# Every second piece of the second expert weights split by GpSimd and ScalarE instead of VectorE

## The chip, the cores and the metric

The kernel runs on one core of one Trainium2 chip. Its engines are TensorE (PE in the profile, with its weight loads as PEld), VectorE (DVE), ScalarE (ACT), GpSimd (POOL) and SyncE (SP), which here only issues DMAs. The metric is the device time in microseconds. The kernel before took 1023.83 us as the median of three runs (1018.97 to 1024.21). One execution was profiled; it took 1020.09 us, of which 1018.3 us lie between its first and its last instruction.

## The reference

Three layers follow one another. Attention over 4 batches, 8 heads and 576 positions with a bias made by a small network from the positions; a mixture of 8 experts, in which each token goes to the one expert that it is nearest to; and a feed-forward layer with a squared ReLU.

```python
scores = scale * np.matmul(q, k.transpose(0, 1, 3, 2)) + bias.transpose(2, 0, 1)[None]
attn = softmax(scores); x = (attn @ v) as rows (2304, 512)
for e in range(8):                       # the experts
    h = np.maximum(x[mask] @ w1[e], 0.0)
    out[mask] = gate_w[mask, None] * (h @ w2[e])
h = x @ w_in; g = np.maximum(h, 0.0) ** 2
return g @ w_out
```

The change touches only how `w2` is prepared.

## The kernel before

The kernel is written for one order per engine: each engine runs its instructions in the order in which the program issues them, and waits on semaphores for the others. Attention comes first (roughly 40 to 380 us), then the experts in slots of 128 tokens, then the feed-forward layer.

Attention is one loop over half-steps, `hs`. A half-step is one head of one 128-row block: the scores of head `hs + 1` on TensorE (`emit_qk`, L498), the bias sum and the maximum of head `hs` on VectorE (`emit_max`, L509), the exponential of head `hs - 1` on ScalarE (`emit_exp`, L522), the transposes of head `hs - 3` on TensorE (L531) and their copies out of PSUM (`copy`, L207 on ScalarE or L209 on VectorE), and the product with `v` (L556). The scores have two PSUM buffers, so TensorE can write the scores of head `hs + 1` only once VectorE has read those of head `hs - 1`.

Everything else in that stretch runs as generators, which are resumed once per half-step, at its end: the making of the bias (`bias_group`, whose first ReLU of four goes to GpSimd at L324), the preparation of `q` and `k`, the row sums and the routing of finished rows (`rows`, `route`, L594 to L717), and `presplit`, which is the subject here. A `yield E_` means "go on at the end of the next half-step". Two running totals, `load["A"]` for ScalarE and `load["D"]` for VectorE, stand for the work handed to each engine; they fall by `STEP = 1.95` per half-step. `pick` gives a copy or a ReLU to the engine with the smaller total, `room` holds a generator back while a total would go over `LIM = 2.7`, and `A` and `V` add to a total. So an instruction that is moved from one engine to another also moves copies and ReLUs between VectorE and ScalarE.

`presplit(i)` runs for 32 pieces of `w2`, 128 x 1024 numbers each, and makes of each two half-precision parts, a high one and the remainder: it loads the piece (L465), waits three half-steps, has GpSimd write the high half, `wh[:, 0] = 64 * wr` (L471), waits two half-steps, has VectorE write the remainder, `wh[:, 1] = 64 * wr - wh[:, 0]` (L475), and stores both (L479). There are two `wr` and two `wh` buffers, so two pieces are under way at most. The experts load these parts back later.

## Time and profile before

| what | value |
|---|---|
| median of three runs | 1023.83 us |
| profiled execution | 1020.09 us, span 1018.3 us |
| TensorE busy | 946.7 us (93%) |
| VectorE busy | 662.0 us (65%) |
| ScalarE busy | 540.9 us (53%) |
| GpSimd busy | 499.1 us (49%) |
| L471 on GpSimd | 32 times, 62.2 us |
| L475 on VectorE | 32 times, 47.1 us |

The shares are means over the whole span; the stages differ. The pieces are split between 85 and 345 us, and what the change is worth has to be read there: how busy each engine is in that stretch, and which engine TensorE waits for. Idle time of an engine that nobody waits for costs nothing.

### The profile page before, as it was taken

What the parts mean: (1) busy time and instruction counts of PE and PEld (TensorE: products, weight loads), DVE (VectorE), ACT (ScalarE), POOL (GpSimd) and SP (SyncE); (2) the same over time, 40 slices, a digit from 0 to 9 for tenths busy, and PEclk for the clock granted to TensorE, in tenths of its full rate; (3) what the DMA queues carried; (4) which work ended last, traced back from release to release, by engine and by line L of the source; (5) the groups of instructions that cost most, each with busy time, mean ns of one, the idle gap of its engine ahead of it and who ended that gap; (6) DMA issues with size and microseconds to landing.
All of it is one profiled execution on the core that took longest, in us unless ns stands there. A gap on an engine that the chain in (4) does not pass through costs nothing. (4 is left out here: it accounts for less than half of the span.)

```text
span 1018.3 us, 24810 instructions
## 1 busy us (share of the span) xinstructions
PE 946.7 (93%) x9725; PEld 747.8 (73%) x9725; DVE 662.0 (65%) x1229; ACT 540.9 (53%) x1000; POOL 499.1 (49%) x415
## 2 busy tenths in 40 slices
PE   8687988999899889999999899999999999999995
PEld 4355766677577767776666667688888888888884
DVE  6655899888997874677776767245446455545441
ACT  5666776767777683467565555255423333233330
POOL 1212536446534353366548797275454554645631
PEclk9789999999999999999999999999999999999998
DMA  9998885898779434599899484462011111111000
GB/s 296 318 254 264 305 279 179 267 268 286 226 234 330 163 126 176 213 338 334 325 361 340 146 291 151 153 258 53 22 54 43 32 52 43 32 53 22 22 12 32
DMA packets 78843, 187.17 MB, mean 184 GB/s; under 512 B 26648, under 2 KB 26776, under 8 KB 76128
## 3 DMA queue, kind: packets, MB, share of 16 engines
q1 hardware_dynamic: 72656, 169.98, 49.5%
q0 software_dynamic: 6064, 15.54, 4.4%
q8 instruction: 78, 1.28, 0.5%
q14 instruction: 45, 0.37, 0.1%
HBM read 171.65 MB, written 51.73 MB: 219 GB/s over the span
## 5 line engine op out<-in xcount | busy, mean ns | idle before, releaser
L1436 POOL TENSOR_TENSOR gf<-gf 128x256 f32<-128x256 f32 x144 | 166.0, 1172 | 131.0 <-DVE gf L1433 108.8
L1420 PE MATMUL pf<-big,wih 128*128 128x256 f16 x1728 | 196.0, 273 | 1.5 <-PEq L1374 1.5
L1420 PEld LDWEIGHTS <-wih 128*128 128x128 f16 x1728 | 169.0, 98 | 21.6 <-issue 2.0
L1458 PEld LDWEIGHTS <-g 128*128 128x128 f16 x1512 | 147.4, 98 | 18.7 <-issue 1.0
L1426 ACT ACTIVATE gf<-pf 128x512 f32<-128x512 f32 x72 | 42.5, 597 | 193.3 <-PE pf L1420 140.3
L1220 PE MATMUL ph<-x,w1b 128*128 128x128 f16 x2112 | 127.5, 220 | 7.9 <-DVEq L1024 3.0
L1220 PEld LDWEIGHTS <-w1b 128*128 128x128 f16 x2112 | 122.0, 99 | 13.1 <-DVEq L1024 3.5
L471 POOL TENSOR_TENSOR wh<-wr,w2s_c 128x1024 f16<-128x1024 f32 x32 | 62.2, 1943 | 135.9 <-DMA wr<-in_mw_dram 65.0
L1235 PE MATMUL py<-vt,h 128*128 128x512 f16 x528 | 119.4, 383 | 3.8 <-DMA vt<-wsc 3.8
L1444 DVE TENSOR_TENSOR g<-gf,g 128x1792 f16<-128x1792 f32 x36 | 85.5, 2374 | 50.1 <-ACT g L1443 50.1
L522 ACT ACTIVATE pr<-ssb,mn 128x576 f32<-128x576 f32 x144 | 111.7, 776 | 10.3 <-DVE mn L509 10.3
L509 DVE CUSTOM_DVE_ANT_0 ssb<-ps_s,bias 128x576 f32<-128x576 f32 x144 | 107.4, 749 | 3.1 <-DMA bias<-bias_d 2.2
L1433 DVE TENSOR_TENSOR gf<-gf 128x1024 f32<-128x1024 f32 x28 | 34.3, 1226 | 113.6 <-ACT gf L1426 113.6
L498 PE MATMUL ps_s<-kst,qd 128*128 128x288 f16 (+1 forms) x640 | 96.6, 292 | 11.7 <-DVE mn L509 9.2
L1235 PEld LDWEIGHTS <-h 128*128 128x128 f16 x528 | 51.3, 99 | 63.0 <-issue 7.0
L531 PE MATMUL ps_t<-cst,pr 128*128 128x128 f32 x576 | 92.1, 283 | 2.5 <-DVE pl L607 1.3
L531 PEld LDWEIGHTS ps_t<-cst,pr 128*128 128x128 f32 x576 | 64.9, 144 | 25.7 <-issue 20.8
L556 PE MATMUL pv<-pt,vt 128*64 128x128 f32 (+1 forms) x1280 | 83.6, 274 | 0.0
L498 PEld LDWEIGHTS <-qd 128*128 128x128 f16 (+1 forms) x640 | 56.2, 101 | 26.6 <-issue 16.4
L556 PEld LDWEIGHTS pv<-pt,vt 128*64 128x64 f32 x1280 | 65.5, 140 | 12.5 <-issue 11.4
L1226 DVE SCALAR_TENSOR_TENSOR h<-ph,h 128x512 f16<-128x512 f32 x44 | 30.3, 690 | 49.9 <-ACT h L1225 35.0
L1443 ACT CAST g<-gf 128x1792 f16<-128x1792 f32 x36 | 60.3, 1676 | 4.4 <-POOL gf L1436 4.4
(194 smaller groups left out, 1571.9 us busy)
## 6 DMA issues: line engine op xcount, KB each, us to landing
vt<-wsc SPq DMA_DIRECT2D x88, 512.0 KB
wr<-in_mw_dram SPq DMA_DIRECT2D x76, 512.0 KB
kst<-in_mw_dram SPq DMA_DIRECT2D x44, 512.0 KB
wsc<-wh SPq DMA_DIRECT2D x32, 512.0 KB
bias<-bias_d SPq DMA_DIRECT2D x16, 576.0 KB
bias_d<-rt SPq DMA_DIRECT2D x28, 295.5 KB
qd<-qh SPq DMA_DIRECT2D x64, 128.0 KB
wr<-in_win_dram SPq DMA_DIRECT2D x8, 1024.0 KB
```

The source lines that it names most:

```text
L471: POOL.tensor_tensor(out=wh[:, 0], in0=wr, in1=w2s_c.to_broadcast([P, 1024]), op=ALU.mult)
L498: PE.matmul(s[r, hf, :288], lhsT=qd[:, h2, i, pr, r], rhs=kst[x - x % 2][:, pr, h2, x % 2, js], start=(i == 0), stop=(i == 1))
L509: DVE.tensor_tensor_reduce(out=ss.rearrange("p (a j) -> p a j", a=2), in0=s[:, :, :288], in1=btile[bkey[u]][:, h2].rearrange("p (a j) -> p ...
L522: ACT.activation(pr_sb[k_ // 2][:, h2], ssb.pop(k_), AF.Exp, bias=mns.pop(k_), scale=-1.0, accum_out=sums[c, b][:, h:h + 1])
L531: PE.transpose(pt_ps[k_][:, jc * P:(jc + 1) * P], src[:, j0:j0 + P], eye)
L556: PE.matmul(pv[o, cs], lhsT=vb[:, 2 * jc + h2, d] if jc < 4 else vb[o, 8, d], rhs=a[h2][:, jc, cs] if jc < 4 else e[o, cs], start=(jc == 4 ...
L1220: PE.matmul(p_[:, f4, :], lhsT=w[:, a, kc, f * P:(f + 1) * P], rhs=x2[:, b, kc, :], start=(i == 0), stop=(i == 11))
L1235: PE.matmul(p_, lhsT=h2[:, a, fc, :], rhs=wb2[fc // 2][:, b, fc % 2, :], start=(i == 0), stop=(i == 23))
L1420: PE.matmul(p_[:, h], lhsT=wih[:, a, kc, f * P:(f + 1) * P], rhs=y2[:, b, kc, :], start=(i == 0), stop=(i == 11))
L1436: POOL.tensor_tensor(out=g[:, d], in0=g[:, x], in1=g[:, y], op=op)
L1444: DVE.tensor_tensor(out=gt[:, 1, :, c:c + 2, :], in0=g[:, 1:8], in1=gt[:, 0, :, c:c + 2, :], op=ALU.subtract)
L1458: PE.matmul(ps, lhsT=gt[:, a, s, c, :], rhs=woh[:, c, b, w, :], start=(i == 0 and first), stop=(i == 23 and end), skip_group_check=True)
```

## The change

Pieces of even number go as before, with three differences: the wait after the load is two half-steps instead of three, `room` asks for 1.5 instead of 1.2, and VectorE's total grows as if by 1400 columns instead of 1024. Pieces of odd number go another way: GpSimd multiplies the piece by 64 in place (`wr = 64 * wr`), one half-step later ScalarE copies it into the high half, and GpSimd subtracts the high half from it into the remainder. The wait after the load is two half-steps there too.

```diff
-            for _ in range(3):
+            for _ in range(2):
                 yield E_
             yield from take("wh")
 ...
-            POOL.tensor_tensor(out=wh[:, 0], in0=wr, in1=w2s_c.to_broadcast([P, 1024]), op=ALU.mult)
-            for _ in range(2):
-                yield E_
-            yield from room("D", 1.2)
-            DVE.scalar_tensor_tensor(out=wh[:, 1], in0=wr, scalar=s, in1=wh[:, 0], op0=ALU.mult, op1=ALU.subtract)
-            V(1024)
-            yield E_
+            if i % 2:
+                POOL.tensor_scalar(wr, wr, s, 1.0, op0=ALU.mult, op1=ALU.mult)
+                yield E_
+                yield from room("A", 1.0)
+                ACT.copy(wh[:, 0], wr)
+                A(1024)
+                POOL.tensor_tensor(out=wh[:, 1], in0=wr, in1=wh[:, 0], op=ALU.subtract)
+                yield E_
+                yield E_
+            else:
+                POOL.tensor_tensor(out=wh[:, 0], in0=wr, in1=w2s_c.to_broadcast([P, 1024]), op=ALU.mult)
+                for _ in range(2):
+                    yield E_
+                yield from room("D", 1.5)
+                DVE.scalar_tensor_tensor(out=wh[:, 1], in0=wr, scalar=s, in1=wh[:, 0], op0=ALU.mult, op1=ALU.subtract)
+                V(1400)
+                yield E_
             give("wr")
             SP.dma_start(out=wsc2[i * P:(i + 1) * P, :], in_=wf)
```

The file grows by ten lines, so what stands below the change has a line number that is ten higher after it (L509 becomes L519, L522 becomes L532); of the pieces themselves, L471 becomes L481 and L475 becomes L485, and the new lines are L472 (GpSimd's multiplication in place), L475 (ScalarE's copy) and L477 (GpSimd's subtraction).

TensorE's order doesn't change. On VectorE, counted over the whole program, 16 of the 32 instructions of L475 go; 5 copies of 512 columns, 4 copies `pte` and 5 copies `big` of 128 columns come over from ScalarE, and 3 bias evictions (L335). ScalarE gets 16 copies of 1024 columns and gives up as many of the small ones. GpSimd loses 16 instructions of L471 and gets 16 multiplications and 16 subtractions.

The first place is the routing of the rows of batch group (0, 0), near 150 us. On VectorE, before, from the maximum of one head (L509, with its accumulator read) to the end of the half-step; L651 and L653 are two short steps of the routing.

```order
L509 ISA ssb,mn<-ps_s,bias 128x576
L509 ISA mn 128x1
L475 SCALAR_TENSOR_TENSOR wh<-wr,wh 128x1024
L651 TENSOR_TENSOR z<-z,zm 128x32
L653 TENSOR_SCALAR eq<-z 128x32
```

The same half-step on VectorE now.

```order
L519 ISA ssb,mn<-ps_s,bias 128x576
L519 ISA mn 128x1
L661 TENSOR_TENSOR z<-z,zm 128x32
L663 TENSOR_SCALAR eq<-z 128x32
L326 TENSOR_SCALAR rt<-u_t,bcol 128x320
```

The remainder of an odd piece is gone from before the routing step; a ReLU of the bias has come over from ScalarE behind it.

On ScalarE, before, from the exponential of the next head (L522), with the copies of transposed heads (`pt`, `pte`) and of a finished product (`big`).

```order
L522 ACTIVATE pr,sums<-ssb,mn 128x576
L207 COPY pt<-ps_t 128x512
L207 COPY big<-pv 128x128
L522 ACTIVATE pr,sums<-ssb,mn 128x576
L207 COPY pte<-pv 128x128
```

The same on ScalarE now.

```order
L532 ACTIVATE pr,sums<-ssb,mn 128x576
L207 COPY pt<-ps_t 128x512
L475 CAST wh<-wr 128x1024
L207 COPY big<-pv 128x128
L532 ACTIVATE pr,sums<-ssb,mn 128x576
L207 COPY pt<-ps_t 128x512
```

The copy of an odd piece into its high half now stands ahead of `big` and of the next exponential, and it needs GpSimd's multiplication to be done.

The second place is on GpSimd, a little later: two pieces (L471), the ReLU of a bias group (L324), and the indirect DMAs that write the tokens' places (L701).

```order
L471 TENSOR_TENSOR wh<-wr,w2s_c 128x1024 x2
L324 TENSOR_SCALAR rt<-u_t,bcol 128x304
L701 DMA id_d<-tok,ri 296960x1 x3
L324 TENSOR_SCALAR rt<-u_t,bcol 128x320
L701 DMA id_d<-tok,ri 296960x1
```

The same place on GpSimd now, where L481 is the high half of an even piece, L472 and L477 the multiplication and the subtraction of an odd one, and L711 the indirect DMAs.

```order
L481 TENSOR_TENSOR wh<-wr,w2s_c 128x1024
L472 TENSOR_SCALAR wr<-wr 128x1024
L324 TENSOR_SCALAR rt<-u_t,bcol 128x304
L711 DMA id_d<-tok,ri 296960x1 x2
L477 TENSOR_TENSOR wh<-wr,wh 128x1024
L711 DMA id_d<-tok,ri 296960x1
L324 TENSOR_SCALAR rt<-u_t,bcol 128x320
```

An odd piece now has two instructions on GpSimd, and what stands between and behind them waits for ScalarE's copy as the subtraction does.

## Rows read from the trace of the kernel before

**Rows 1.** Busy time per engine in three stretches (columns: engine busy us, instructions)

```profile
85.00:345.00 260.00, 238.38 (x2637) 176.80 (x2636) 224.08 (x570) 184.67 (x474) 120.63 (x69) 0.99 0.80 258
140.00:160.00 20.00, 15.47 (x170) 11.64 (x170) 19.83 (x38) 12.08 (x33) 8.92 (x5) 1.00 0.74 229
700.00:800.00 100.00, 100.00 (x918) 89.36 (x917) 51.23 (x53) 33.95 (x43) 51.93 (x45) 1.00 0.17 45
```

**Rows 2.** TensorE's waits for VectorE, 85 to 345 us (total, times, longest)

```profile
PE ps_s L498 <- DVE mn L509: 6.7, 7, 2.1
...
PE rk L670 <- DVE oh L662: 2.9, 2, 2.0
PE pv L536 <- DVE big L209: 2.0, 3, 1.2
PE ps_t L531 <- DVE pl L607: 1.3, 1, 1.3
PE ps_t L531 <- DVE pt L209: 1.0, 2, 0.8
```

**Rows 3.** The split's two instructions: busy us, mean ns; for L475 also min/median/max

```profile
L471 POOL TENSOR_TENSOR wh<-wr,w2s_c 128x1024 f16<-128x1024 f32 x32 | 62.2, 1943 | 135.9 <-DMA wr<-in_mw_dram 65.0 <-DMA kst<-wh 32.5 <-DVE pt L209 10.3
L475 DVE SCALAR_TENSOR_TENSOR wh<-wr,wh 128x1024 f16<-128x1024 f32 x32 | 47.1, 1472 | 4.7 <-POOL wh L471 4.7
...
L475 DVE SCALAR_TENSOR_TENSOR wh<-wr,wh x32: 1209/1222/2862, 92.2 to 332.9; 128x1024 f16<-128x1024 f32 x32
```

**Rows 4.** Timeline near 150 us (start us, duration us, engine; idle before in brackets)

```profile
149.62 2.28 POOL L471 TENSOR_TENSOR wh<-wr,w2s_c 128x1024 f16<-128x1024 f32 x1 [4.21 <-DMA wr<-in_mw_dram]
...
150.06 1.88 DVE L651 TENSOR_TENSOR z<-z,zm 128x32 f32<-128x32 f32 x1
...
153.16 0.65 PE L498 MATMUL ps_s<-kst,qd 128*128 128x288 f16 x4 [2.06 <-DVE mn L509]
...
154.80 1.90 POOL L471 TENSOR_TENSOR wh<-wr,w2s_c 128x1024 f16<-128x1024 f32 x1 [0.19 <-DMA wr<-in_mw_dram]
...
154.91 2.86 DVE L475 SCALAR_TENSOR_TENSOR wh<-wr,wh 128x1024 f16<-128x1024 f32 x1
```

**Rows 5.** Two short VectorE operations, each by its line (ns min/median/max)

```profile
L651 DVE TENSOR_TENSOR z<-z,zm x6: 171/187/1884, 150.1 to 398.2; 128x32 f32<-128x32 f32 x3, 128x16 f32<-128x16 f32 x3
...
L326 DVE TENSOR_SCALAR rt<-u_t,bcol x76: 328/464/2011, 5.4 to 278.7; 128x576 f32<-128x576 f32 x6, 128x352 f32<-128x352 f32 x6, 128x560 f32<-128x560 f32 x5, 128x544 f32<-128x544 f32 x5
```

**Rows 6.** Operations like the new ones, from later stages

```profile
L1038 POOL TENSOR_TENSOR xs<-xg,xs 128x512 f16<-128x512 f32 x22 | 28.6, 1302 | 1.8
...
L1037 POOL TENSOR_SCALAR xg<-xg 128x512 f32<-128x512 f32 x22 | 21.8, 990 | 48.7 <-ACT xs L1036 40.5 <-PE ph L1220 7.9
...
L1014 ACT ACTIVATE w1b<-wr x20: 1044/1048/1065, 360.4 to 575.3; 128x1024 f16<-128x1024 f32 x20
```

**Rows 7.** VectorE's groups between 85 and 345 us (busy us, mean ns)

```profile
L509 DVE CUSTOM_DVE_ANT_0 ssb<-ps_s,bias 128x576 f32<-128x576 f32 x109 | 81.4, 748 | 0.6 <-PE ps_s L498 0.5
...
L209 DVE COPY pt<-ps_t 128x512 f32<-128x512 f32 x33 | 22.6, 686 | 13.6 <-PE ps_t L531 13.6
...
L209 DVE COPY pte<-pv 128x128 f32<-128x128 f32 x16 | 4.6, 290 | 3.4 <-PE pv L536 3.1
```

**Rows 8.** Two loads of a piece, each followed by GpSimd's start; GpSimd's wait in total

```profile
158.19 0.43 SPq L465 DMA_DIRECT2D wr<-in_mw_dram  x1
...
162.62 1.90 POOL L471 TENSOR_TENSOR wh<-wr,w2s_c 128x1024 f16<-128x1024 f32 x1 [5.92 <-DMA wr<-in_mw_dram]
...
195.25 0.44 SPq L465 DMA_DIRECT2D wr<-in_mw_dram  x1
...
201.16 1.89 POOL L471 TENSOR_TENSOR wh<-wr,w2s_c 128x1024 f16<-128x1024 f32 x1 [6.17 <-DMA wr<-in_mw_dram]
...
POOL wh L471 <- DMA wr<-in_mw_dram: 65.0, 20, 9.3
```

**Rows 9.** ScalarE's longest wait in total, 85 to 345 us (total, times, longest)

```profile
ACT big L207 <- PE pv L556: 26.6, 35, 7.3
```

## The prediction

> **What bounds the kernel now.** I read the windows first, then TensorE's waits, then the two instructions of the split, then one stall in order of time. After 700 us TensorE is busy without a gap [rows 1], so a microsecond won or lost in attention arrives at the end as it is; nothing there depends on when attention ended. The pieces are split between 85 and 345 us. In these 260 us TensorE is busy 238.4, VectorE 224.1, ScalarE 184.7 and GpSimd 120.6 us [rows 1]. So TensorE bounds the stretch, VectorE is close behind, and only the 260 - 238.4 = 21.6 us in which TensorE idles can be won. The waits say whose they are: for VectorE 6.7 + 2.9 + 2.0 + 1.3 + 1.0 = 13.9 us [rows 2], which is the most that a lighter VectorE can give. They come in clusters: between 140 and 160 us VectorE is busy for 19.83 of 20 us and TensorE for only 15.47 [rows 1].
>
> One cluster shows how they arise [rows 4]. At 149.62 GpSimd starts the high half of a piece. At 150.06 VectorE starts a subtraction of 32 columns, which takes 1.88 us instead of its usual 0.19 [rows 5] and ends within 0.1 us of GpSimd's instruction (149.62 + 2.28 = 151.90). The maximum behind it is late, and TensorE waits 2.06 us for it. At 154.91 the remainder of a piece starts 0.11 us behind another GpSimd instruction and takes 2.86 us. So VectorE is late not only by what it has to do, but also by what GpSimd does beside it.
>
> **The change part by part.** A half-step is 260 / 109 = 2.39 us (109 maxima of L509 in the stretch [rows 7]).
>
> *GpSimd.* Sixteen high halves of 1.943 us go [rows 3], 31.1 us. Sixteen multiplications in place and sixteen subtractions come. The nearest rows have half the columns: 0.990 and 1.302 us [rows 6], doubled 1.98 and 2.60 us, together 16 x 4.58 = 73.3 us. Net +42 us, from 120.6 to 163 us of 260, a third more (35%). There is room for it, so by itself it costs nothing; what it costs is through VectorE and ScalarE, below.
>
> *VectorE.* The remainder takes 1.222 us when nothing is in its way and 1.472 in the mean [rows 3], so (1.472 - 1.222) x 32 = 8.0 of its 47.1 us are delay. Sixteen stay: 16 x 1.222 = 19.6, and half the delay, raised by GpSimd's 35%, 4.0 x 1.35 = 5.4, together 25.0, which is 22.1 less. Against it: five copies of 512 columns at 0.686 and nine of 128 at 0.290 [rows 7], 3.4 + 2.6 = 6.0; three bias evictions, at most 0.686 each, 2.1; and more delay of the short operations that GpSimd holds up, such as the 1.88 and 2.01 us beside medians of 0.19 and 0.46 [rows 5]. How much that is in total no single row says; I take it as large as that of the remainders, 8.0, and 35% of it as added, 2.8. The bounds are 0 and double that. Net 22.1 - 10.9 = 11.2 us less, 5% of 224.1.
>
> The Trainium skill, SBUF — State Buffer, section "SBUF: two separate sides", says that VectorE and GpSimd share one pair of ports as an exclusive lock, that a VectorE operation with two inputs from SBUF and a GpSimd operation that reads SBUF shut each other out for a whole instruction, and that one with its input in PSUM isn't touched. The timeline agrees, with the subtraction that ended with GpSimd's instruction [rows 4]. The rule speaks against this change: an odd piece, which VectorE no longer works on, still shuts VectorE's routing steps out, for longer than before. By the rule the 2.8 us belong in the sum; without it they would be 0, and VectorE 14.0 us lighter.
>
> What that is worth to TensorE: the bounds are 0 and all 13.9 us. Half of the remainders go, so a remainder disappears from ahead of about half of these waits, 6.9 us; 10.9 of the 22.1 us come back in other places, half, and so I take -3.5 us. I don't go further because TensorE is short of work only in clusters, and the routing steps that make them stay where they are.
>
> *ScalarE.* Sixteen copies of 1024 columns at 1.048 us [rows 6] are 16.8 us, less than its idle time of 260 - 184.7 = 75.3 us, part of which goes in copies to VectorE. It is ahead of TensorE much of the time (26.6 us of waiting for a finished product [rows 9]). That cover hides the copies themselves. But each copy is also a new wait. It stands three half-steps behind the load's issue (two after the load, one more after the multiplication), 3 x 2.39 = 7.2 us, unless `room` holds it longer. A piece lands 4.4 to 5.9 us after its issue (162.62 - 158.19 and 201.16 - 195.25 [rows 8]), and the multiplication takes 1.98: 6.4 to 7.9 us. So ScalarE stands still for 0 to 0.7 us at a copy, with the next exponential and the next copy of transposed scores queued behind it, for which TensorE's product with `v` waits. At 0.35 us each that is 5.6 us of ScalarE, of which its lead hides most; I take +1.5 us. Below it is 0; above it is the second rival.
>
> *The queues.* The loads of later pieces are issued by SyncE behind the stores of earlier ones as before; a store of an odd piece now waits for GpSimd instead of VectorE. Behind that store stand loads of bias rows and of `q`, which the program issues 6 and 15 half-steps ahead of their use, and I cost this at 0; without that lead a late store would delay a half-step by as much as GpSimd is late, the second rival's price. The shorter wait after the load makes GpSimd stand waiting for the piece earlier than today, where it waits 65.0 us for pieces already [rows 8]; the ReLU of a bias group behind it starts later, against some half-steps of slack.
>
> *Sum.* -3.5 + 1.5 = -2 us on the profiled execution: 1020.1 - 2 = 1018.1. The median of the three runs is 3.7 us above that execution; I put the base between the two, at 1022, and forecast 1020.
>
> **The rivals.**
>
> *VectorE's waits go nearly all.* For it: VectorE is full just where TensorE stands still, and a cluster goes once VectorE is ahead by its length; the longest wait is 2.1 us [rows 2], less than one delayed remainder of 2.86 [rows 4]. Against it: the routing steps stay, with more GpSimd beside them. Then -13.9 + 1.5 = -12.4, which is 1010.
>
> *GpSimd gets in ScalarE's way.* GpSimd works in order, and a multiplication can stand behind another instruction of the pieces or of a bias group, about 1.94 us (the mean of L471 [rows 3]). Then ScalarE waits 0.35 + 1.94 = 2.3 us at its copy, and with about 1 us hidden by its lead TensorE loses 1.3. It decides as soon as ScalarE waits over 1 us at a copy in the mean. For it: GpSimd's third more work, and the subtraction, which waits for ScalarE in turn, so that each holds up the other. Against it: GpSimd is idle for 260 - 163 = 97 us even then. If half of the copies meet it, 8 x 1.3 = 10.4, and if all do, 21; with VectorE's -3.5 the first is +7, which is 1029, slower than before.
>
> *VectorE gets no lighter.* The delays by GpSimd and the copies that come over take back all 22.1 us: if the short operations lose not 2.8 but 14 us more. Then 0 + 1.5 gives 1023, no change.
>
> **How the numbers follow.** The forecast has a chance of 0.44, with a range of its own from 1015 to 1026; VectorE's waits gone 0.28; GpSimd in ScalarE's way 0.21; VectorE no lighter 0.07. What a measurement of this kernel can tell from no change is about 0.5%, 5 us: the runs before differ by that. Faster by more has the second case and a little of the first, 0.32; slower by more the third and a little of the first, 0.23; within it 0.45. The range takes in most of both sides, 1010 to 1030.
>
> **What would show it.** In the profile of the changed kernel, 16 remainders on VectorE with a mean near 1.5 us; GpSimd near 163 us busy in the same stretch; VectorE 5% less busy there, with TensorE's waits for it near 10 instead of 13.9 us; ScalarE waiting for GpSimd at its new copies, under 1 us each. The forecast is wrong if TensorE's waits for VectorE fall below 5 us, or if ScalarE's waits for GpSimd go over 16 us in total, 1 us per copy.

## The result, and the profile after

The changed kernel takes 1034.03 us, the median of six runs (1030.04 to 1042.68), beside 1021.40 us for the kernel before on the same chip (six runs, 1015.85 to 1024.66): a ratio of 1.0137 over all runs (1.0124 by the medians), with a 95% interval of [1.0106, 1.0167]. The change costs about 13 us; the prediction was 1020 us and its range ended at 1030. The profiled execution took 1032.69 us with a span of 1030.9 us, 12.6 us more than before's 1018.3 us, so it is a fair sample of the difference.

The windows of the changed kernel in the three stretches of [rows 1] come first (engine busy in the order PE, PEld, DVE, ACT, POOL; then the granted clock, DMA share and GB/s).

```profile
85.00:345.00 260.00, 237.81 (x2536) 174.73 (x2535) 203.86 (x536) 186.86 (x454) 138.28 (x82) 0.95 0.81 254
140.00:160.00 20.00, 15.45 (x157) 11.51 (x158) 15.45 (x40) 13.42 (x34) 10.62 (x6) 0.97 0.88 286
700.00:800.00 100.00, 100.00 (x918) 89.45 (x917) 51.02 (x53) 39.59 (x50) 51.72 (x46) 1.00 0.17 44
```

VectorE looks much lighter, 203.86 instead of 224.08 us, and in the cluster at 140 to 160 us 15.45 instead of 19.83. Yet TensorE is busy for as long as before and issues 101 instructions fewer in the same 260 us (2536 instead of 2637), and its granted clock is 0.95 instead of 0.99. The 260 us hold less of the work than before, so the engines' times in them can't be compared as they stand.

So the stretch has to be cut by its work and not by its time. Half-steps 24 to 143 run from 93.4 to 379.4 us before and from 95.8 to 391.9 us after. That window of the kernel before:

```profile
93.40:379.40 286.00, 261.41 (x2859) 193.82 (x2861) 245.49 (x634) 204.50 (x521) 139.15 (x88) 0.98 0.75 247
```

And of the changed kernel:

```profile
95.80:391.90 296.10, 271.32 (x2859) 200.47 (x2861) 232.28 (x634) 214.27 (x523) 158.68 (x103) 0.95 0.74 235
```

Both hold the same 2859 instructions on TensorE, in the same order. Over them VectorE is 245.49 - 232.28 = 13.2 us lighter, and GpSimd 158.68 - 139.15 = 19.5 us heavier. TensorE idles for 286.0 - 261.4 = 24.6 us before and 296.1 - 271.3 = 24.8 us after, so its stops are no longer in total. The same instructions take 9.9 us more. These 9.9 us, 2.4 us by which half-step 24 starts later (95.8 - 93.4), and the 0.2 us of idling are 12.5 of the 12.6 us.

Nearly all of the 9.9 us lies where the clock differs. Before, the stretches of this part at the lower of the two levels (0.50, which is 1.2 instead of 2.4 GHz) are these.

```profile
97.00:103.80 6.80, 5.13 (x32) 4.16 (x33) 1.45 (x2) 1.31 (x5) 4.34 (x3) 0.50 0.48 192
370.00:373.40 3.40, 3.40 (x25) 2.21 (x24) 3.37 (x5) 1.52 (x4) 3.07 (x5) 0.51 0.01 2
```

After, there are six of them.

```profile
97.20:104.00 6.80, 6.11 (x36) 4.88 (x37) 2.43 (x3) 2.67 (x8) 3.64 (x3) 0.50 0.88 337
158.60:165.40 6.80, 6.34 (x51) 3.92 (x51) 5.80 (x11) 3.49 (x10) 5.34 (x3) 0.50 0.67 192
257.60:261.00 3.40, 3.40 (x29) 2.05 (x28) 0.58 (x3) 1.26 (x4) 3.06 (x3) 0.50 0.83 315
329.30:336.10 6.80, 6.80 (x43) 6.13 (x42) 2.47 (x8) 3.48 (x11) 3.13 (x3) 0.50 0.85 286
349.80:353.20 3.40, 3.40 (x24) 2.74 (x21) 1.10 (x4) 1.03 (x3) 0.00 (x0) 0.50 0.00 0
377.10:380.50 3.40, 3.40 (x25) 2.62 (x24) 1.90 (x3) 3.22 (x6) 3.30 (x5) 0.50 0.76 297
```

That is 30.6 us at half rate instead of 10.2 (30.7 where the edges aren't rounded, as in the table below). If TensorE does half as much in the 20.4 us between them, it needs 10.2 us more, close to the 9.9 measured. The instructions say the same one by one: the 163 that begin at full clock before and at half clock after add 24.1 instead of 13.6 us to TensorE's busy time, the 23 for which it is the other way 1.9 instead of 3.3, and the 2641 at full clock in both 240.2 instead of 239.4.

The first and the last of the six stretches have one like them before; the other four are new, 20.4 us in all. Each of the four comes with a stop of TensorE: 158.6 with one of 3.93 us and 329.3 with one of 1.99, both for a copy of ScalarE, 257.6 with one of 1.97 for a maximum and 349.8 with one of 1.39 for the routing, both for VectorE. So 13.6 of the 20.4 us stand behind ScalarE and 6.8 behind VectorE. TensorE's waits between 85 and 345 us show which stops are new (total, times, longest; these answer to [rows 2]).

```profile
PE ps_s L508 <- DVE mn L519: 8.8, 7, 2.4
PE pv L546 <- ACT big L207: 6.8, 4, 3.9
PE pv L566 <- DMA vt<-in_v_dram: 2.7, 1, 2.7
PE pv L546 <- DVE big L209: 1.5, 2, 1.1
PE ps_t L541 <- DVE rt L335: 1.0, 1, 1.0
```

The waits for VectorE here are 8.8 + 1.5 + 1.0 = 11.3 us, and 12.7 with 1.4 for the routing's `rk` behind 345 us, instead of 13.9 before. New is the second row: the transpose L546, which writes into the tile `pv`, waits for ScalarE's copy `big`, up to 3.9 us in one piece. Before, there is no such row in this window. Over half-steps 24 to 143 it grows from the first of these to the second:

```profile
PE pv L536 <- ACT big L207: 1.8, 2, 1.3
...
PE pv L546 <- ACT big L207: 9.2, 6, 3.9
```

Over the same half-steps the waits for VectorE fall from 16.4 to 12.3 us and the wait for `v`'s load from 6.4 to 2.7. That is why the idle time comes out equal: the new waits for ScalarE stand in the place of others.

The longest of the new waits in order of time, on the changed kernel (start us, duration us, engine; idle before in brackets):

```profile
149.74 0.44 SPq L465 DMA_DIRECT2D wr<-in_mw_dram  x1
...
152.25 2.08 POOL L481 TENSOR_TENSOR wh<-wr,w2s_c 128x1024 f16<-128x1024 f32 x1 [4.77 <-DVE eq L666]
...
154.32 2.42 POOL L324 TENSOR_SCALAR rt<-u_t,bcol 128x320 f32<-128x320 f32 x1
...
156.71 1.05 POOL L472 TENSOR_SCALAR wr<-wr 128x1024 f32<-128x1024 f32 x1
...
157.79 1.04 ACT L475 CAST wh<-wr 128x1024 f16<-128x1024 f32 x1 [4.07 <-POOL wr L472]
158.74 0.26 ACT L207 COPY big<-pv 128x128 f32<-128x128 f32 x1
...
159.06 0.47 PE L546 MATMUL pv<-cst,pr 128*128 128x128 f32 x1 [3.93 <-ACT big L207]
```

Read it from the bottom. TensorE's next transpose writes into `pv`, which has one buffer in PSUM, and waits 3.93 us until ScalarE has copied the last product out of it (`big`). `big` stands on ScalarE right behind the new copy, and the copy waits 4.07 us for GpSimd. GpSimd had to do the high half of another piece and a bias ReLU first (L481, L324), back to back, and only then the multiplication. Before L481 it had idled for 4.77 us itself; the load of that piece had been issued 7.4 us ahead of it, at 144.82. At 158.6, while TensorE stands, the clock falls.

The other long wait for ScalarE behind which the clock falls, near 327 us, has another start:

```profile
317.47 0.45 SPq L465 DMA_DIRECT2D wr<-in_mw_dram  x1
...
325.15 1.05 POOL L472 TENSOR_SCALAR wr<-wr 128x1024 f32<-128x1024 f32 x1 [2.71 <-DVE pl L617]
326.23 1.04 ACT L475 CAST wh<-wr 128x1024 f16<-128x1024 f32 x1 [3.72 <-POOL wr L472]
...
327.50 0.33 PE L546 MATMUL pv<-cst,pr 128*128 128x128 f32 x1 [1.99 <-ACT big L207]
```

Here GpSimd does nothing for 2.71 us before the multiplication, whose load was issued 7.7 us ahead of it. (The row names a step of VectorE that doesn't touch the piece.) The two other waits of ScalarE for a multiplication, 2.62 us at 233.04 and 1.73 us at 311.61, are of this kind too: GpSimd had idled for 7.77 and 3.65 us, by their rows for the load, which it could use 7.4 and 7.0 us after its issue.

ScalarE's waits, 85 to 345 us, on the changed kernel:

```profile
ACT big L207 <- PE pv L566: 17.3, 24, 3.0
...
ACT wh L475 <- POOL wr L472: 12.1, 4, 4.1
...
ACT wh L475 <- DMA kst<-wh: 3.0, 1, 3.0
```

Only five of the 16 copies wait, but for 3 us each in the mean. ScalarE's cover, its wait for a finished product, is down from 26.6 [rows 9] to 17.3 us, and over half-steps 24 to 143 from 30.7 to 23.8. GpSimd waits for ScalarE in return, as its row in the same stretch shows.

```profile
POOL wh L477 <- ACT wh L475: 35.7, 15, 5.0
```

The instructions of the split on the changed kernel (duration in ns, min/median/max), which answer to [rows 3]:

```profile
L472 POOL TENSOR_SCALAR wr<-wr x16: 1038/1048/1888, 92.6 to 334.6; 128x1024 f32<-128x1024 f32 x16
...
L475 ACT CAST wh<-wr x16: 1032/1048/1056, 94.6 to 339.7; 128x1024 f16<-128x1024 f32 x16
...
L477 POOL TENSOR_TENSOR wh<-wr,wh x16: 2126/2139/2154, 95.8 to 340.8; 128x1024 f16<-128x1024 f32 x16
...
L485 DVE SCALAR_TENSOR_TENSOR wh<-wr,wh x16: 1214/1222/2681, 91.2 to 344.3; 128x1024 f16<-128x1024 f32 x16
```

### The profile page after: what moved, and what is told of

Its sections match the earlier page's. It is cut to its first block, busy times and chain, and to the rows that moved or that the text cites. A ratio compares the mean times of both kernels' runs of the same rounds, so it can differ in the third digit from the quotient of the medians.

```text
span 1030.9 us, 24844 instructions
## 1 busy us (share of the span) xinstructions
PE 957.4 (93%) x9725; PEld 755.2 (73%) x9725; DVE 648.5 (63%) x1230; ACT 550.5 (53%) x999; POOL 521.2 (51%) x431
## 5 line engine op out<-in xcount | busy, mean ns | idle before, releaser
L1230 PEld LDWEIGHTS <-w1b 128*128 128x128 f16 x2112 | 122.1, 99 | 12.3 <-DVEq L1034 3.1
L532 ACT ACTIVATE pr<-ssb,mn 128x576 f32<-128x576 f32 x144 | 111.6, 775 | 6.2 <-DVE mn L519 5.9
L519 DVE CUSTOM_DVE_ANT_0 ssb<-ps_s,bias 128x576 f32<-128x576 f32 x144 | 107.4, 748 | 4.8 <-DMA bias<-bias_d 2.4
L541 PE MATMUL ps_t<-cst,pr 128*128 128x128 f32 x576 | 95.3, 290 | 1.5 <-DVE rt L335 1.0
L566 PE MATMUL pv<-pt,vt 128*64 128x128 f32 (+1 forms) x1280 | 87.2, 281 | 0.1
L541 PEld LDWEIGHTS ps_t<-cst,pr 128*128 128x128 f32 x576 | 67.2, 148 | 25.8 <-issue 19.7
L566 PEld LDWEIGHTS pv<-pt,vt 128*64 128x64 f32 x1280 | 68.3, 144 | 13.0 <-issue 11.6
L1453 ACT CAST g<-gf 128x1792 f16<-128x1792 f32 x36 | 60.3, 1676 | 4.4 <-POOL gf L1446 4.4
L481 POOL TENSOR_TENSOR wh<-wr,w2s_c 128x1024 f16<-128x1024 f32 x16 | 30.9, 1932 | 61.4 <-DMA qraw<-in_q_dram 27.0
```

What stands on the lines that cost most here:

```text
L519: DVE.tensor_tensor_reduce(out=ss.rearrange("p (a j) -> p a j", a=2), in0=s[:, :, :288], in1=btile[bkey[u]][:, h2].rearrange("p (a j) -> p ...
L532: ACT.activation(pr_sb[k_ // 2][:, h2], ssb.pop(k_), AF.Exp, bias=mns.pop(k_), scale=-1.0, accum_out=sums[c, b][:, h:h + 1])
L541: PE.transpose(pt_ps[k_][:, jc * P:(jc + 1) * P], src[:, j0:j0 + P], eye)
L566: PE.matmul(pv[o, cs], lhsT=vb[:, 2 * jc + h2, d] if jc < 4 else vb[o, 8, d], rhs=a[h2][:, jc, cs] if jc < 4 else e[o, cs], start=(jc == 4 ...
L1230: PE.matmul(p_[:, f4, :], lhsT=w[:, a, kc, f * P:(f + 1) * P], rhs=x2[:, b, kc, :], start=(i == 0), stop=(i == 11))
L1453: ACT.copy(gt[:, 0, :, c:c + 2, :], g[:, 1:8])
```

## The experiments

The theory after the first comparison: the price is the new wait of ScalarE at its copy, which the single `pv` buffer hands on to TensorE at once, together with the lower clock behind each such stop. The rival: GpSimd's longer work on an odd piece holds up VectorE and the bias, and the wait at the copy is a side effect.

One table for all of them. The ratio is to runs of the kernel before on the same chip. The next columns are of the one profiled execution, in half-steps 24 to 143: length, TensorE busy, what is left as idle, time at a granted clock of 0.50, and VectorE's delay (the excess of each of its instructions over the lower quartile of its own line and shape in the whole profile, summed). The last column is over the whole span and the mean of all runs: time at half rate, worked out as 2 x (1 - mean granted clock) x span, less the same for the runs of the kernel before in that session, which lay between 44.4 and 48.1 us.

| kernel | ratio, interval | length | busy | idle | at 0.50 | VectorE's delay | half rate, all runs |
|---|---|---|---|---|---|---|---|
| before | 1 | 286.0 | 261.4 | 24.6 | 10.2 | 29.7 | 0 |
| changed | 1.0137 [1.0106, 1.0167] | 296.1 | 271.3 | 24.8 | 30.7 | 28.0 | (60.3 in all) |
| e1 ScalarE first | 1.0131 [1.0062, 1.0200] | 298.7 | 268.0 | 30.7 | 22.8 | 26.7 | +15.3 |
| e2 no odd way | 1.0039 [1.0006, 1.0072] | 290.6 | 267.9 | 22.7 | 21.6 | 27.3 | +4.2 |
| e3 wait alone | 1.0108 [1.0055, 1.0162] | 302.4 | 271.3 | 31.1 | 30.7 | 25.4 | +12.6 |
| e4 all on GpSimd | 1.0261 [1.0190, 1.0331] | 319.7 | 275.8 | 43.9 | 44.8 | 46.2 | +25.2 |
| e5 no GpSimd | 1.0067 [1.0027, 1.0108] | 283.2 | 261.4 | 21.8 | 8.9 | 10.3 | +10.5 |
| e9 copy later | 1.0176 [1.0136, 1.0216] | 297.4 | 269.6 | 27.8 | 29.0 | 34.0 | +16.4 |
| e10 filler | 1.0172 [1.0127, 1.0217] | 295.3 | 269.1 | 26.2 | 23.7 | 24.9 | +14.4 |
| e12 no GpSimd, old wait | 1.0043 [1.0007, 1.0079] | 281.0 | 260.3 | 20.7 | 11.4 | 13.7 | +3.6 |

A single execution scatters by some 10 us (e12's twelve runs lie between 1018.79 and 1032.34), so a profile's length alone ranks nothing; e5 and e12 were profiled in executions below their medians, and only the ratios rank the kernels.

### First round: which of the parts

**e1.** ScalarE writes the high half straight from the loaded piece, so that it no longer waits for GpSimd; GpSimd's two instructions follow.

```diff
-                POOL.tensor_scalar(wr, wr, s, 1.0, op0=ALU.mult, op1=ALU.mult)
                 yield E_
                 yield from room("A", 1.0)
-                ACT.copy(wh[:, 0], wr)
+                ACT.activation(wh[:, 0], wr, AF.Copy, scale=s)
                 A(1024)
+                POOL.tensor_scalar(wr, wr, s, 1.0, op0=ALU.mult, op1=ALU.mult)
                 POOL.tensor_tensor(out=wh[:, 1], in0=wr, in1=wh[:, 0], op=ALU.subtract)
```

> The changed kernel, but in odd pieces ScalarE writes the high half straight from the loaded piece (scaled by 64), and GpSimd multiplies and subtracts behind it: the same work on each engine, but ScalarE no longer waits for GpSimd. Theory A (ScalarE's wait for GpSimd's multiplication, 12.1 us in 4 waits, stops TensorE, and each stop is followed by a stretch at half clock): TensorE's waits for ScalarE fall from 7 us to under 1, the half-clock time between 110 and 345 us falls from 17 us to about 3, and the time from 1034 to 1021-1026 us. Theory B (GpSimd's longer occupation holds up VectorE): TensorE's waits for VectorE stay near 13 us, and the time stays at 1030-1036. Theory C (the shorter wait after the load and the new load figures, which shuffle copies and ReLUs between ScalarE and VectorE): 1030-1036.

The time did not come back: 1.0131. ScalarE now waits for the load itself, at the same places. Its row between 85 and 395 us:

```profile
ACT wh L474 <- DMA wr<-in_mw_dram: 10.7, 4, 3.4
```

And TensorE's:

```profile
PE pv L546 <- ACT big L207: 7.3, 6, 2.4
PE ps_b L426 <- POOL rt L324: 3.4, 1, 3.4
```

So the copy comes too early for its load, not only for GpSimd: e1 takes away the wait for GpSimd, but not the wait at the copy. The last row is new: two GpSimd instructions in a row push the bias ReLU back by 3.4 us in one place.

**e2.** The odd way is switched off (`if i % 2:` becomes `if False:`): all remainders are on VectorE, odd pieces keep before's figures, and what stays of the change is the shorter wait after the load and the new figures for even pieces.

> The changed kernel without the odd path: all 32 remainders on VectorE again, with the shorter wait after the load, and with the new load figures for even pieces. Theories A and B: as the kernel before, 1017-1025 us. Theory C: 1028 us or more.

1.0039 [1.0006, 1.0072]: if the parts add up, about 0.4% of the 1.4% belongs to the shorter wait and these figures, the rest to the odd way. With the shorter wait, pieces and routing fall on other half-steps; half-step 24 starts at 98.4 us here, at 95.8 in the changed kernel and at 93.4 before.

**e3.** The kernel before, with ScalarE made to wait for GpSimd and little else: in odd pieces, whose wait after the load is one half-step shorter, it copies four columns of the high half, one half-step behind GpSimd.

```diff
-            for _ in range(3):
+            for _ in range(2 if i % 2 else 3):
                 yield E_
 ...
-            for _ in range(2):
-                yield E_
+            yield E_
+            if i % 2:
+                ACT.copy(smp.tile([P, 4], F32, name="dm"), wh[:, 0, :4])
+            yield E_
```

> The kernel before, with one thing added: in odd pieces ScalarE copies 4 columns of GpSimd's high half, one half-step behind the multiplication (and the wait after the load is two half-steps in odd pieces, as in the changed kernel). No work moves, only the wait is there. Theory A: 1028-1036 us, with 3 to 5 waits of ScalarE for GpSimd of 2 to 5 us, TensorE idle behind them, and half clock behind those. Theory B: as before, 1018-1024 us.

1.0108 for a wait with nearly no work behind it. ScalarE's row between 85 and 395 us:

```profile
ACT dm L474 <- POOL wh L471: 32.6, 12, 6.5
```

And TensorE's in the same stretch:

```profile
...
PE pv L538 <- ACT big L207: 4.6, 4, 2.3
...
PE ps_t L533 <- ACT rt L333: 2.0, 1, 2.0
```

The wait, together with the shorter wait after the load of odd pieces, is enough for three quarters of the loss. What the second of them costs without the first was not run; in e2, where it is there for all pieces and with new figures besides, it is 0.39%. And ScalarE's wait here is far longer than in the changed kernel (32.6 against 15.1 us). So e3 makes it likely that such a wait costs, and doesn't show that it is all of the 1.4%.

**e4.** No ScalarE: GpSimd does all three steps of an odd piece (the high half, the multiplication in place, the subtraction).

> The changed kernel, but odd pieces go over GpSimd alone: high half, multiplication in place, subtraction. ScalarE has no copy and no wait, GpSimd has 16 x 1.9 = 31 us more than in the changed kernel. Theory A: 1018-1026 us, since ScalarE waits for nobody. Theory B: slower than the changed kernel, 1035-1042 us, with VectorE's delays and TensorE's waits for VectorE up by about a quarter.

1.0261, the slowest of all, without any wait at a copy. TensorE's waits between 85 and 395 us:

```profile
PE ps_s L506 <- DVE mn L517: 16.9, 10, 3.3
PE ps_b L426 <- POOL rt L324: 6.3, 4, 4.5
```

GpSimd is busy for 189.1 instead of 158.7 us, VectorE's delay grows from 28.0 to 46.2 us, and TensorE waits for VectorE and for the bias. So the rival has a share too: time on GpSimd costs through VectorE's delay and through the ReLU behind it.

**e5.** ScalarE writes the high half, VectorE the remainder, GpSimd nothing of an odd piece (with the shorter wait and before's figures). The odd way, against the kernel before, without the lines behind it:

```diff
+            if i % 2:
+                yield E_
+                yield from room("A", 1.0)
+                ACT.activation(wh[:, 0], wr, AF.Copy, scale=s)
+                A(1024)
+                yield E_
+                yield from room("D", 1.2)
+                DVE.scalar_tensor_tensor(out=wh[:, 1], in0=wr, scalar=s, in1=wh[:, 0], op0=ALU.mult, op1=ALU.subtract)
```

> Odd pieces without GpSimd: ScalarE writes the high half straight from the loaded piece, VectorE the remainder as in the kernel before (all pieces with the old load figures, wait of two half-steps). GpSimd has 31 us less than in the kernel before, VectorE as much, ScalarE 16.8 us more; ScalarE waits for the load alone. If GpSimd beside VectorE is what makes TensorE stop (theory B): VectorE's delays fall by a third, TensorE's waits for VectorE fall below 12 us, half-clock time in attention stays near 10 us, and the time is 0 to 8 us under the kernel before. If ScalarE's longer list is what matters (theory A in its wider form): TensorE's waits for ScalarE rise to 6 us or more, and the time is 5 to 12 us over it.

VectorE's delay falls from 28.0 to 10.3 us, so two thirds of it come with GpSimd's part of the odd pieces. The ratio halves to 1.0067 but does not go below one: what VectorE gains does not pay for the rest. Which part of the half came back with GpSimd's work, and which with before's figures and the shorter waits of ScalarE (3.5 us for loads in 4 places, 3.1 us once for another DMA), this run doesn't tell.

### Second round: `pv` and the places

**e6, e7, e8.** `pv` as two halves of its PSUM bank, in the changed kernel, in the kernel before, and in e5, so that TensorE need not wait for `big`.

```diff
+        pv2 = pvp.tile([P, 2, 2 * P], F32, name="pv")
 ...
-            x = pv_ps[k_ // 2] = pvp.tile([P, 2 * P], F32, name="pv")
+            x = pv_ps[k_ // 2] = pv2[:, k_ // 2 % 2]
```

> The changed kernel with two buffers for the product with v (two halves of its PSUM bank in turn), so that the transposes into the next one no longer wait for ScalarE's copy of the last. ScalarE still waits for GpSimd. If ScalarE's lateness reaches TensorE by that single buffer: TensorE's waits of L546 for big fall from 6.8 to under 1 us, the half-clock stretches behind them go (about 14 of 30.7 us), and the time falls by 8 to 14 us against the changed kernel, to 1.000-1.005 of before. If it reaches TensorE by the exponential and the copies as well: the waits turn up at the transposes or at the product, and the time falls by under 4 us.

> The kernel before with the same two buffers. TensorE waits there for ScalarE's big for only 2.3 us and for VectorE's for 2.0 us in attention. If stops of TensorE cost the clock besides: up to 4 us less by the waits, and 0 to 4 us by the clock, 0.992-0.999 of before. If they are too short to matter: the same within 0.3%.

> Both: odd pieces by ScalarE and VectorE without GpSimd, and two buffers for the product with v. Theory B with the single buffer as ScalarE's way to TensorE: the fastest of the four, 0.988-0.996 of before, with half-clock time in attention at 10 us or less. If VectorE's own work sets the waits: as e7.

e6 gave 1.0169 [1.0118, 1.0219], e7 0.9989 [0.9958, 1.0019], e8 1.0087 [1.0055, 1.0119]. TensorE's row in e6 shows why this decides nothing:

```profile
PE pv L547 <- ACT big L208: 10.8, 6, 4.1
```

The wait did not go away, so the edit didn't do what it was meant to; why, no run shows. The Trainium skill, PSUM — Partial Sum Buffer, section "PSUM bank collisions raise a hardware error", says that the compiler orders any two instructions of different engines that touch the same bank and quadrant one behind the other, which would fit, since both halves lie in one bank; no run here shows it. The two halves are also parts of one tile of the program, which could have the same effect. A second bank was not tried, since all eight are in use. What e6 does show is that the stops repeat: 4.07 us at half-step 48, 1.97 at 86 and 2.03 at 117, where the changed kernel has 3.93, 1.97 and 1.99. The slow stretches behind them do not all repeat: behind the second and the third, for which the changed kernel has 3.4 and 6.8 us at half rate, e6 has none (granted clock 1.00 from 165.9 to 370.5 us).

**e9.** The changed kernel with ScalarE's copy two half-steps later (`yield E_` three times instead of once in front of it).

> The changed kernel with ScalarE's copy two half-steps later, five behind the load, where VectorE's remainder stood in the kernel before. ScalarE's waits for GpSimd or for the load should be gone (15.1 us in the changed kernel to under 2), and with them TensorE's stops in half-steps 48, 78, 110 and 117. If the too early copy is what made the change slower: half-clock time in attention falls from 30.7 to 10-17 us and the time to 0.997-1.004 of before. If GpSimd's longer occupation matters as much: stops by VectorE and by GpSimd's late ReLU remain or come in their place, and the time is 1.006-1.012 of before.

ScalarE's waits at the copy are gone (0.3 us), and the time is not: 1.0176. TensorE's waits between 85 and 395 us:

```profile
PE ps_s L509 <- DVE mn L520: 14.7, 14, 5.1
PE ps_b L426 <- POOL rt L324: 3.5, 2, 2.2
PE pv L547 <- DVE big L209: 3.4, 3, 2.8
PE pv L547 <- ACT big L207: 3.1, 2, 2.8
```

This is what refutes the simple form of the theory. With the copy out of the way, stops as long (5.1, 2.8, 2.2 us) appear behind VectorE and GpSimd, at other half-steps, and VectorE's delay is 34.0 us. The stop of 2.8 us for ScalarE, in half-step 136, comes when the pieces are done; the changed kernel has one of 1.98 us there and the kernel before one of 1.32.

**e10.** The changed kernel with idle matmuls in front of three of the transposes that wait, to keep TensorE active through the stop.

```diff
+            for _ in range({48: 30, 110: 16, 116: 16}.get(now[0], 0)):
+                PE.matmul(s_ps[k_ + 4][:, 1, 384:512], lhsT=one16, rhs=one16, start=True, stop=True)
```

> The changed kernel with 62 matrix products of no use in front of the transposes at which TensorE stops: 30 in half-step 48, 16 each in 110 and 116. They work only where TensorE would stand still. If the stop itself is what lowers the clock: the stretches at half clock behind these stops (6.8 us each at 158.6 and 329.3 us) are gone, TensorE's busy time counts the filling, and the time falls by 3 to 8 us against the changed kernel (ratio to before 1.006-1.010). If the clock falls for another reason: the stretches stay, and the time is the changed kernel's or up to 3 us above it.

The stretches at half rate behind half-steps 48 and 117 shrink from 6.8 to 3.4 us each, and the total from 30.7 to 23.7 us. The stop in half-step 48 is shorter, 2.51 instead of 3.93 us; the one in 117 is not, 2.06 beside 1.99 us, with 1.06 us of idle matmuls in front of it. The time does not follow: 1.0172, with a stop of 5.19 us at half-step 136 where the changed kernel has one of 1.98. So work put in front of a stop went with a shorter slow stretch behind it, but that this clock is worth 10 us in the changed kernel is not shown by this run.

**e11.** The kernel before, with `v` loaded earlier for the last two batches (at half-steps 14 and 17 instead of 16 and 20), against the longest stop that both kernels have (6.4 us before).

> The kernel before with its largest stop taken away: the loads of v of batches 2 and 3 are issued 2 and 3 half-steps earlier, so that TensorE doesn't wait 6.4 us for them in half-step 24. If a stop costs its length and the half clock behind it (6.8 us at half speed): 5 to 9 us less than before, 0.991-0.995. If the loads of the keys or of the pieces are pushed back by it: the stop moves to them, and the time is within 0.3% of before.

The stop goes, and 1.0003 [0.9976, 1.0030]: in its place stand shorter ones for VectorE at half-steps 24 to 26 (the longest 2.79 us). Half-step 24 also starts at 97.6 instead of 93.4 us. Removing one wait again brought out the next.

### Third round: the lighter VectorE without a wait at the copy

**e12.** e5 with before's wait of three half-steps after the load. Against the kernel before, only the high half of the odd pieces moves, from GpSimd to ScalarE, one half-step later.

> Odd pieces: ScalarE writes the high half from the loaded piece, VectorE the remainder, GpSimd nothing; and every piece waits three half-steps after its load, as in the kernel before. Against the variant of the same split with a wait of two half-steps (1.0067 [1.0027, 1.0108]) only that wait changes. Theory (what costs time is that an engine stands still at the copy for a load or for another engine, and the stops that TensorE then makes): ScalarE's waits for the load (3.5 us there, 4 times) go to under 1 us, GpSimd's for the pieces shrink, and the time is the kernel before's within 0.5%, ratio 0.995 to 1.005; VectorE's delay by GpSimd stays near 10 us instead of near 28, and if that is worth anything the ratio is below 0.998. Rival (ScalarE's added microsecond itself, in front of the copies that TensorE waits for, is the price): the ratio stays at 1.005 to 1.010, with TensorE's waits for ScalarE at 4 us or more between 85 and 385 us.

ScalarE no longer waits for a load at its copy (one wait of 2.3 us for another DMA stays), and TensorE hardly for ScalarE. TensorE's waits between 85 and 385 us:

```profile
PE ps_s L509 <- DVE mn L520: 11.9, 11, 2.2
...
PE pv L547 <- ACT big L207: 1.0, 1, 1.0
```

1.0043 [1.0007, 1.0079], within the band that the theory gave; the rival's waits for ScalarE (4 us or more) are not there. VectorE is 11.0 us less busy than before (234.5 against 245.5) over these half-steps and its delay is 13.7 instead of 29.7 us, yet TensorE's wait for its maxima is 11.9 us, where it was 9.2 before. What this kernel still loses, about 0.4%, is not located; its interval overlaps e5's, so that the wait alone made the difference between them isn't proved either.

No version beat the kernel before: e7 and e11 are equal to it, the others slower.

## Why the prediction was wrong

**What bounds the kernel** held: TensorE bounds the stretch, a microsecond lost there arrives at the end (the changed kernel is 12.5 us late from the end of attention on, and after 700 us TensorE is busy without a gap as in [rows 1]).

**GpSimd's price** was too high, which does not decide the outcome, since the sum takes GpSimd's own time at nothing. The multiplication in place, put at 1.98 us from the 512-column row of [rows 6], takes 1.05; the subtraction 2.14 instead of 2.60. The mean of that row, 990 ns, holds delays, which the kernel before shows by the row's spread (ns, min/median/max):

```profile
L1037 POOL TENSOR_SCALAR xg<-xg x22: 686/696/2645, 363.6 to 620.4; 128x512 f32<-128x512 f32 x22
```

Twice the median would have been 1.39. GpSimd's busy time grew by 19.5 us over half-steps 24 to 143, not by 42. Its order of work did matter in one place: the chain near 150 us has three of its instructions in a row while it idles elsewhere.

**VectorE** held. It got lighter by 13.2 us over half-steps 24 to 143, where 11.2 was put (the 20.2 us by which the 260 us differ hold less work), and the remainders that stayed take a median of 1.222 us as put. TensorE's waits for it fell by 4.1 us over these half-steps, from 16.4 to 12.3, where 3.5 was put. That a lighter VectorE brings little was right; in e12 it is lighter too, and its maxima are waited for longer. Its delay stayed about where it was, 28.0 beside 29.7 us; one row shows how GpSimd's subtraction now does to it what the high half did in [rows 4]. On the changed kernel:

```profile
299.90 2.14 POOL L477 TENSOR_TENSOR wh<-wr,wh 128x1024 f16<-128x1024 f32 x1 [2.13 <-ACT wh L475]
299.95 2.11 DVE L726 TENSOR_SCALAR gt<-rne 128x2 f32<-128x2 f32 x1
...
302.86 0.53 PE L508 MATMUL ps_s<-kst,qd 128*128 128x288 f16 x3 [1.65 <-DVE mn L519]
```

A step of two columns takes 2.11 us, where the median of its line is 0.16, and ends with GpSimd's instruction (299.90 + 2.14 = 302.04, 299.95 + 2.11 = 302.06); the maximum behind it is late and TensorE waits 1.65 us. The Trainium skill, SBUF — State Buffer, section "SBUF: two separate sides", says that GpSimd's instruction and a VectorE step in a two-port mode, or with two inputs from SBUF, exclude each other for a whole instruction. The trace agrees with its 2.11 us; which of the two conditions this step meets is not shown here.

**ScalarE** is the first step that failed, and in it first the term for the load. "A piece lands 4.4 to 5.9 us after its issue" was read from the two loads of [rows 8]. The trace of before had more: in the 20 places where GpSimd waited for a load, it started 4.2 to 8.1 us after the issue, in six of them more than 7.0. One of these:

```profile
115.51 0.39 SPq L465 DMA_DIRECT2D wr<-in_mw_dram  x1
...
123.01 1.90 POOL L471 TENSOR_TENSOR wh<-wr,w2s_c 128x1024 f16<-128x1024 f32 x1 [4.09 <-DMA wr<-in_mw_dram]
```

With a multiplication of 1.05 us a copy 7.2 us behind the issue comes in time only if the multiplication can start within 6.15 us of it, and in ten of the 20 places GpSimd started later. On the changed kernel the four multiplications that ScalarE waits for start 7.0 to 7.7 us after their load's issue, three of them with GpSimd idle just before and one, near 150 us, behind two other instructions of GpSimd. So "ScalarE stands still for 0 to 0.7 us at a copy" became 0 for eleven of the 16 copies and 1.7 to 4.1 us for five, 12.1 + 3.0 = 15.1 us in all. And "of which its lead hides most" overlooked what stands behind the copy: `big`, for which the single `pv` buffer makes TensorE wait at once. The lead did hide the wait of 2.62 us; of those of 4.07 and 3.72 us it left TensorE 3.93 and 1.99. In place of the +1.5 us, TensorE's waits for ScalarE grew by 7.4 us for `big` over half-steps 24 to 143 (1.8 to 9.2).

The second rival, at 0.21 and 1029 us, had the sign and a wait of ScalarE at the copy that reaches TensorE, but its cause, a multiplication that stands behind other work of GpSimd, is that of one wait of the four, and a slower clock is not in its 1029 us. The measure by which it was to be told, more than 1 us per copy in the mean or 16 us in total, misses it: 15.1 us stay under it, and two of the waits make both new stops.

**The sum** is the second step that failed. It counted waits and took an instruction of TensorE as equally long before and after. By waits alone it came out nearly right, TensorE's idle time in half-steps 24 to 143 being 24.8 instead of 24.6 us where -2 was foreseen, but that is luck: the waits for ScalarE grew by about five times the +1.5, and the wait for `v`'s load, which the prediction doesn't name, gave back 3.7 us (6.4 to 2.7). It did so because TensorE came to it later: in front of half-step 24 stands a new stop of 2.37 us for a maximum at 94.5 us, behind a remainder and six steps of the row sums, and TensorE goes on behind `v`'s load at 97.89 us, where it was 98.67 before. What was missing is the 9.9 us by which the same 2859 instructions are slower, beside 30.6 instead of 10.2 us at half rate; in [rows 1] the granted clock was still 0.99, and no term of the sum is for the clock. The Trainium skill, TensorE: Matmul & The Clock Gate, section "HAM oscillation — how this bites in real kernels", says that TensorE's waits between pieces of work can let the clock fall, so that the next piece starts at half rate. The trace agrees for the stops of 3.93, 1.97 and 1.99 us on the changed kernel. It shows too that not every stop does so: behind those of 2.06 us at 153.2 [rows 4] and 2.00 us at 336.8 us before, the clock stayed at 1.00.

How much of the loss is the clock? In the profiled execution 9.9 of 12.6 us. Over all runs the changed kernel has 60.3 us at half rate, 12 to 16 more than the 44.4 to 48.1 of before in the other sessions, which at half of it is 6 to 8 of 13 us. The rest is not seen in this profile; it must lie in longer stops or elsewhere in the other executions. In the experiments the same count gives about half of the added time: e4 12.6 of 26.8 us, e1 7.7 of 13.4, e3 6.3 of 11.1 (the ratio's excess times the median of before); in e5 it is more, 5.3 of 6.9. That fewer or shorter stops bring the clock up, and with it the time, was tried once, in e10; the clock came up and the time did not follow.

**What is shown, what stays open.** Shown on the profiled executions: the same instructions of TensorE take 9.9 us longer, nearly all of it where the clock is lower, and two thirds of the new slow time stand behind two waits for ScalarE, the rest behind two for VectorE. Shown by runs: more of GpSimd's time on a piece costs more (e4, with longer waits for VectorE and the bias), and without GpSimd's part, with before's figures again, about half of the loss is gone (e5; more of it in e12, with before's wait as well). A wait of ScalarE with next to no work costs 1.1% together with a shorter wait after the load (e3), and the shorter wait with the new figures some 0.4% (e2); the share of each is not separated. Refuted: that the time comes back once the wait at the copy goes; in e9 it is gone, and the loss is no smaller. (e1 is no test of it, since there ScalarE waits at the copy for the load.) Open: whether the changed kernel would be as fast as before at the full clock, why one stop of 2 us lowers the clock and another does not, how e9's loss divides between VectorE's delay and GpSimd's queue, whether a `pv` of its own bank would hide the wait, and what the last 0.4% of e12 is.

## What to carry to other kernels

When an instruction is moved to an engine that has room, look not only at its idle time but at what stands right behind the instruction there, and whether the bounding engine has a second buffer to go on with meanwhile; one long wait can cost where the mean says nothing. Read how long a load takes from all its rows and not from two, and price the late ones. Where the bounding engine is TensorE, price each new stop with the slow stretch that may follow it, and compare the two kernels over the same instructions and not over the same time. A chain in which two engines wait for each other in turn (multiplication, copy, subtraction) binds three queues together; in these runs, removing one of its waits brought out the next.

## What the runs showed of the hardware

- GpSimd's multiplication in place by constants takes a median of 1.048 us for 128 x 1024 numbers and 0.696 us for 128 x 512: it doesn't double with the columns, and the first is half as long as its subtraction of two tensors (2.139 us).
- A VectorE step with a single tensor input of two columns took 2.11 us, to the end of GpSimd's subtraction beside it, where the median of its line is 0.16. With GpSimd's part taken out of the odd pieces VectorE's delay over half-steps 24 to 143 fell from 28.0 to 10.3 us (e5).
- In half-steps 24 to 143 the stretches at the lower clock last 3.4 or 6.8 us in the profiles of the table (10.2 in two places of e4).
- The length of a stop of TensorE did not decide whether one follows: behind stops of 1.97 and 1.99 us on the changed kernel the granted clock fell to 0.50, behind those of 2.06 and 2.00 us before, and of 1.97 and 2.03 us at the same half-steps in e6, it stayed at 1.00.
